# Attention at the head of a three-stage kernel: each unit's softmax weights are turned and used a step later, and GpSimd gets a written order

## The chip, the cores and the metric

One NeuronCore of a Trainium2 chip runs the whole program. The metric is the device time of one execution in microseconds (us). Engines are named as in the profile: PE (TensorE matmul), PEld (TensorE weight load), DVE (VectorE), ACT (ScalarE), POOL (GpSimd), SP (SyncE, which issues the DMAs here).

## The reference

Three stages in float32. Sizes: 4 batches, 8 heads, 576 positions, head size 64; then 2304 tokens of width 512, 8 experts of hidden width 1024, and a last layer of hidden width 2048.

```python
# attention: a window of 128 positions behind the query, with a slope per head
scores = q @ k.T / 8
mask = (rel >= 0) & (rel < 128)
scores = where(mask, scores - slope[h] * abs(rel), -1e9)
attn = softmax(scores); x = attn @ v
# mixture of experts: one expert per token, chosen by the largest logit
logits = x @ w_gate + modality_bias[modality_id]
e = argmax(logits); gate = softmax(logits)[e]
x = gate * (relu(x @ w1[e]) @ w2[e])
# last layer
h = x @ w_in; out = (h * cos(h)) @ w_out
```

## The kernel before

The change touches only the attention stage. Its work is cut into 36 units: 2 pairs of batches, 9 tiles of 128 rows each (the fifth of a pair holds the last 64 rows of both batches), 2 groups of four heads. Unit n goes through these parts, each a function:

- `load` (by `ahead`, seven units ahead) brings q, k and v by DMA from SP's queue. q and k lie in a pool of 7 buffers, v in the ring `vts` of 12 tiles.
- `tr` (four units ahead) transposes q and k on PE into a "T" bank (two banks). ACT copies the result (`qT`, `rT`), and POOL makes the high and low halves of k and the low half of q: three POOL instructions (L682 to L684). In the trace these transposes are `bk<-ident,rqk`.
- `score(n)` multiplies q and k on PE (`bk<-kT,qT`). Then DVE merges the diagonal block with its neighbour (L716), adds the bias and takes the minimum (L722), and ACT takes the exponential into `e` (L725). Units with s = 4 (8, 9, 26 and 27) hold three blocks of keys; their e is the tile `e1`, one buffer. The others have two buffers.
- `flip(n)` transposes e on PE (`bk<-ident,e`) into the one "P" bank. ACT copies it (L742), and for most units POOL cuts two triangles out of it with two affine selects (L746, L748) into `pT`.
- `pv(n)` multiplies pT and v on PE (`bk<-vt,pT`) into the one "O" bank. DVE divides by the row sums (L766, L767, L770). After the second head group the rows of x are stored.
- For every tile `xt_split` transposes x and splits it on ACT and DVE. For every second tile `logits` adds three calls: `products` (gate logits on PE, copied by ACT to `ls`), `choose` (two small transposes and a chain of eight small DVE instructions, the last of which writes `ohb`, L825), and `ranks` (seven tiny matmuls on `ohb`, then a DVE chain with the integer casts and shifts L255 to L259, and L218).

The loop over n issues, in one step: score(n), one call from the list `after`, tr(n+4), flip(n-1), pv(n-2), one more call from `after`. So choose runs in the first half of a step, and ranks in the second half of the same step. The class `Turns` makes PE keep this written order in steps 2 to 32; the order of the other engines is the scheduler's. In the first steps `setups` also issues the bias of the three-block units (POOL and DVE), the loads for routing (`load_route`, ten small DMAs, half-step 5), the integer tables (DVE casts of POOL's iotas, L602, half-step 8), and `setup_route` (half-step 11), in which PE transposes a tile `mf` that DVE casts just before.

Of the kernel before, what the change touches and what calls it, by code (L numbers as in the profile page):

```python
# [8 lines left out]
F32 = mybir.dt.float32  # L9
# [20 lines left out]
def kernel(  # L30
# [14 lines left out]
    nc = tc.nc  # L45
    B, H, S, D = q.shape
    NT, DM = out.shape
    NE, _, FF = w1.shape
# [10 lines left out]
    TE = T - 2  # L59
# [13 lines left out]
    def pool(c, name, bufs, side="left"):  # L73
        return c.enter_context(tc.tile_pool(name=name, bufs=bufs, side=side, reuse_waits="tile"))
# [93 lines left out]
    class Steps:  # L168


        def __init__(self, queue):
            self.queue, self.going = queue, []
# [306 lines left out]
    class Turns:  # L479


        on, last = False, None

        def __getattr__(self, name):
            op = getattr(tc.nc.tensor, name)

            def call(*args, **kwargs):
                with ExitStack() as c:
                    if self.on and self.last is not None:
                        c.enter_context(tc.issue_after(self.last.ins))  # L490
                    self.last = op(*args, **kwargs)  # L491
                return self.last

            return call

    class Ordered:

        sync, scalar, vector, gpsimd, tensor = nc.sync, nc.scalar, nc.vector, nc.gpsimd, Turns()

    nc = Ordered  # L500

    with ExitStack() as c:
# [3 lines left out]
        sm = pool(c, "sm", 5)  # L506
        vp = pool(c, "vp", 1)
# [137 lines left out]
        units = [(bp, s, hg) for bp in range(B // 2) for s in range(9) for hg in range(2)]  # L645
        N = len(units)
        R, KT, QT, X, ST, PT, O = {}, {}, {}, {}, {}, {}, {}
        vts = [vp.tile([128, 260], F32, name=f"vt{j}") for j in range(12)]

        def vt_of(bp, s, hg):  # L650
            return vts[(18 * bp + 2 * s + hg) % len(vts)]
# [34 lines left out]
        def score(n):  # L686
            bp, s, hg = units[n]
            t0, nt, bt, bc, f0, nv = window(s)
            if n < 2:
                nt = nv  # L690
            w, w0, wv = 128 * nt, 128 * f0, 128 * nv
            kT, qT = KT[bp, hg][:, :, :, 128 * t0:128 * t0 + w], QT.pop(n)
            nm = sm.tile([128, 4], F32, name="nm")
            e = sm.tile([128, 4, 128 * (3 if nv == 3 else 1)], F32, name="e%d" % (nv // 3), bufs=2 if nv < 3 else 1)

            def products(sc, pairs):


                for p in pairs:
                    for a, b in ((0, 0), (0, 1), (1, 0)):  # L700
                        for j in range(2):
                            rs = slice(64 * j, 64 * j + 64)
                            nc.tensor.matmul(sc[j][:, p - pairs[0], :w], qT[rs, a, p], kT[rs, b, p],
                                             start=a == 0 and b == 0, stop=a == 1)

            for pairs in ([0, 1],) if nv < 3 else ([0], [1]):
                if pairs[0]:
                    yield
                sc = [bank("S", [128, 2, 256] if nv < 3 else [128, 1, 512]) for j in range(2)]
                products(sc, pairs)  # L710
                for j in range(2):
                    if nv == 2:


                        own, other = (slice(128, 256), slice(0, 128)) if s < 4 else (slice(0, 128), slice(128, 256))
                        nc.vector.copy_predicated(sc[j][:, :, other], near.unsqueeze(1).to_broadcast([128, 2, 128]),  # L716
                                                  sc[j][:, :, own])
                        w0, wv, bc = other.start, 128, 0
                    for p in pairs:
                        h = 2 * p + j  # L720
                        x = sm.tile([128, 384], F32, name="sx")
                        MARK["dve"] = nc.vector.tensor_tensor_reduce(  # L722
                            out=x[:, :wv], in0=sc[j][:, p - pairs[0], w0:w0 + wv], in1=bt[:, 4 * hg + h, bc:bc + wv],
                            op0=ALU.add, op1=ALU.min, scale=-0.125, scalar=3.0e38, accum_out=nm[:, h:h + 1])
                        MARK["act"] = nc.scalar.activation(e[:, h, :wv], x[:, :wv], AF.Exp, bias=nm[:, h:h + 1],  # L725
                                                           scale=-1.0)
            ST[n] = (e, nv, t0 + f0)
            yield
# [27 lines left out]
        def pv(n):  # L756
            bp, s, hg = units[n]
            heads, t0 = PT.pop(n)
            ot = bank("O", [128, 4, 128])
            for h, pT in enumerate(heads):  # L760
                for b in range(len(pT)):
                    nc.tensor.matmul(ot[:, h, 0:65], pT[b], vt_of(bp, t0 + b, hg)[:, 65 * h:65 * h + 65],
                                     start=b == 0, stop=b == len(pT) - 1)
            t = 9 * bp + s
            den = sm.tile([128, 4], F32, name="den")
            nc.vector.tensor_scalar(den, ot[:, :, D], 1.0e-9, None, op0=ALU.add)  # L766
            nc.vector.reciprocal(den, den)  # L767
            if hg == 0:
                X[t] = gp.tile([128, DM], F32, name="y") if t >= TE else xp.tile([128, DM], F32, name="xt")
            nc.vector.tensor_tensor(  # L770
                X[t][:, 256 * hg:256 * hg + 256].rearrange("p (h d) -> p h d", d=D), ot[:, :, 0:D],
                den.unsqueeze(2).to_broadcast([128, 4, D]), op=ALU.mult)
            if hg == 1:
                with ExitStack() as w:
                    if t >= TE:
                        w.enter_context(tc.issue_after(MK["w"].ins))
                    nc.sync.dma_start(x_dram[128 * t:128 * t + 128, :], X[t])
                after.append(lambda: xt_split(t))
                if t % 2:
                    after.extend(logits(t - 1))  # L780
                if t == TE - 1:
                    after.extend(early())

        def xt_split(t):
            xT = xTs[(t // 2 + 1) % 2]
            c0 = 128 * (t % 2)
            pt = bank("T", [128, KD, 128])
            for kk in range(KD):
                nc.tensor.transpose(pt[:, kk], X[t][:, 128 * kk:128 * kk + 128], ident)
            nc.scalar.copy(xT[:, 0, :, c0:c0 + 128], pt)  # L790
            nc.vector.tensor_tensor(xT[:, 1, :, c0:c0 + 128], pt, xT[:, 0, :, c0:c0 + 128].bitcast(F32),
                                    op=ALU.subtract)
# [45 lines left out]
                rawc.close()  # L838
                RP.append(pool(bc, "rp", 2, "right"))

        LF, LP = 1, 2
        after = []
        for vt in vts:
            nc.vector.memset(vt.rearrange("p (h e) -> p h e", e=65)[:, :, D:65], 1.0)
        ahead(0, 3, 0)
# [6 lines left out]
            ahead(0, 5, 1)  # L852

        def setups(i):
            if i == 5:
                load_route()
            with behind("dve", "act", "pool"):
                if i == 4:
                    LATER.append(setup_bias(bias4))
                if i == 7:  # L860
                    todo.extend(LATER.pop())
                if i == 8:
                    for fn in tables:
                        fn()
                if i == 11:
                    setup_route()
                for fn in todo[:1 if i > 1 else 2]:
                    todo.pop(0)()

        def pops(count):  # L870
            for _ in range(count):
                if after:
                    after.pop(0)()

        LATER = []
        for n in range(N + LP):
            if n < 3:
                ahead(n, dt=n + 1)
            nc.tensor.on = 1 < n < 33
            scores = score(n) if n < N else iter(())  # L880
            next(scores, None)
            setups(2 * n)
            pops(1 if n < 33 else 2)
            if n > 1:
                ahead(n + 1)
            next(scores, None)
            flips = flip(n - LF) if LF <= n < N + LF else iter(())
            next(flips, None)
            setups(2 * n + 1)
            old = len(after)  # L890
            if n >= LP:
                pv(n - LP)
            next(flips, None)
            pops(min(old, 1) if n < 33 else 2 if n < N + LP - 1 else 1)

    nc = tc.nc
    banks(S=2, T=2, P=2, O=1)
# [131 lines left out]
    class InOrder:  # L1029


        on = False
# [18 lines left out]
    class Engines:  # L1051
        scalar, vector, gpsimd, tensor = (InOrder(e) for e in (nc.scalar, nc.vector, nc.gpsimd, nc.tensor))
        sync, values_load = nc.sync, nc.values_load

    nc = Engines
    with ExitStack() as c:
# [104 lines left out]
        for n in range(len(steps) + LAG):  # L1161
            InOrder.on = ORD <= n < ORE
            if n < len(steps):
                i, f = steps[n]
# [81 lines left out]
    with tc.If(n_units > 1):  # L1246
        with tc.For_i(1, n_units):
# [10 lines left out]
            parts = unit_parts()  # L1258
# [12 lines left out]
    with ExitStack() as c:  # L1271
# [16 lines left out]
        GG, ACC, LAST, PART, LP = {}, {}, [], {}, {0: (fp, 512)}  # L1288
# [63 lines left out]
        last = downs[-TAIL:]  # L1352
# [4 lines left out]
        fetches, loads, sums = {}, {}, {}  # L1357
        for s, (g, f0, f1) in enumerate(segs):
            i0 = order.index((s, f0))
            for j in range(groups[g][1]):  # L1360
                if s and (s == 1 or f0 == 0):
                    at = 0 if s == 1 else i0 - 8
# [67 lines left out]
```

## Time and profile before

| | |
|---|---|
| median of 3 runs | 869.53 us (868.23 to 871.9) |
| the profiled execution | 879.99 us, span 878.3 us |
| PE busy | 818.1 us (93%) |
| DVE busy | 615.6 us (70%) |
| ACT busy | 492.2 us (56%) |
| POOL busy | 198.7 us (23%) |
| mean granted PE clock | 0.965 of full |

Shares are of the span. Attention is the first 214 us or so; the two later stages fill the rest. The profiled execution is 10.5 us above the median of the unprofiled runs. A granted clock of 1.00 is 2.4 GHz and 0.5 is 1.2 GHz; a value between is a mean over a stretch that had both.

### The profile page before, as it was taken

The numbers are of one execution on the slowest core, as the hardware profiler recorded it, in microseconds if no ns is written. First come the engines' busy times: TensorE is split into PE (matmuls) and PEld (weight loads), VectorE is DVE, ScalarE is ACT, GpSimd is POOL, SyncE is SP. The second block draws the span as 40 slices with busy tenths as digits, with TensorE's granted clock in tenths as the row PEclk, the third lists the DMA queues.
The fourth block names the chain that finished last, engine by engine and source line by source line (L and its number), as shares of the span: only waits on it lengthen the run. The fifth ranks groups of instructions, "written<-read, shape, count | busy, mean of one in ns | idle before, by whom it ended". The sixth has DMA issues, their size and how long they took to land. (4 is left out here: it accounts for less than half of the span.)

```text
span 878.3 us, 14760 instructions
## 1 busy us (share of the span) xinstructions
PE 818.1 (93%) x5269; PEld 721.6 (82%) x5269; DVE 615.6 (70%) x1461; ACT 492.2 (56%) x912; POOL 198.7 (23%) x259
## 2 busy tenths in 40 slices
PE   7788888998879999999899999999999999999996
PEld 6677877886879999999897877788788888888895
DVE  3853656665888999999474998898656565555562
ACT  6454555654355667666454676675454555445562
POOL 5542546351012213233000212111404000200000
PEclk9697999997999999999989999999999999999999
DMA  8443443104378888877844223140403000100000
GB/s 172 105 113 83 102 104 91 44 26 163 115 234 285 270 279 280 279 251 237 282 147 129 88 71 118 59 169 0 138 20 106 4 0 10 64 1 0 25 26 24
DMA packets 125136, 103.41 MB, mean 118 GB/s; under 512 B 61726, under 2 KB 105028, under 8 KB 125060
## 3 DMA queue, kind: packets, MB, share of 16 engines
q1 hardware_dynamic: 122099, 92.74, 35.1%
q0 software_dynamic: 2960, 9.70, 3.1%
q8 instruction: 42, 0.69, 0.3%
q14 instruction: 35, 0.28, 0.1%
HBM read 85.90 MB, written 16.52 MB: 117 GB/s over the span
## 5 line engine op out<-in xcount | busy, mean ns | idle before, releaser
L1044 PE MATMUL bk<-hh,s 128*128 128x256 f32 x864 | 119.8, 287 | 9.4 <-ACT y L1044 4.5
L1044 PE MATMUL bk<-xT,s 128*128 128x256 f32 x864 | 116.7, 285 | 4.4 <-ACT xT L1044 2.2
L1044 PEld LDWEIGHTS bk<-hh,s 128*128 128x128 f32 x864 | 110.2, 192 | 11.4 <-DVE y L1044 5.2
L1044 PEld LDWEIGHTS bk<-xT,s 128*128 128x128 f32 x864 | 108.9, 191 | 5.3 <-DVE s L1044 2.3
L1044 POOL TENSOR_TENSOR lf<-lf,mag 128x512 f32<-128x512 f32 x32 | 47.7, 1491 | 287.2 <-DVE mag L1044 262.5
L1044 ACT CAST s<-r 128x1024 fp32r<-128x1024 f32 x72 | 75.2, 1051 | 59.9 <-DMA r<-in_moe_w_dram 40.7
L1044 DVE TENSOR_TENSOR s<-r,s 128x1024 fp32r<-128x1024 f32 x72 | 94.1, 1309 | 18.6 <-ACT s L1044 18.3
L1044 PE MATMUL bk<-yT,wi_a 128*128 128x512 f32 (+1 forms) x480 | 104.3, 368 | 1.2 <-DVE yT L1044 0.8
L1044 PE MATMUL bk<-yT,wi_b 128*128 128x512 f32 (+1 forms) x480 | 105.0, 368 | 0.0
L1044 ACT ACTIVATE r<-r 128x512 f32<-128x512 f32 (+1 forms) x80 | 47.2, 590 | 93.5 <-DVE r L1044 93.5
L1044 PEld LDWEIGHTS bk<-yT,wi_a 128*128 128x128 f32 x480 | 84.0, 189 | 17.1 <-DVE yT L1044 1.1
L1044 PEld LDWEIGHTS bk<-yT,wi_b 128*128 128x128 f32 x480 | 84.7, 188 | 15.7
L1044 PE MATMUL bk<-wo_b,gg 128*128 128x512 f32 x384 | 93.2, 391 | 1.8 <-DVE po L1044 1.1
L1044 DVE TENSOR_TENSOR r<-bk,r 128x512 f32<-128x512 f32 (+1 forms) x80 | 51.0, 637 | 61.6 <-ACT r L1044 61.0
L1044 PE MATMUL bk<-wo_a,gg 128*128 128x512 f32 x384 | 92.4, 389 | 0.5 <-DVE gg L1044 0.5
L1044 PEld LDWEIGHTS bk<-wo_b,gg 128*128 128x128 f32 x384 | 71.6, 188 | 18.2 <-issue 1.3
L1044 PEld LDWEIGHTS bk<-wo_a,gg 128*128 128x128 f32 x384 | 71.9, 188 | 15.9 <-DVE gg L1044 1.0
L491 PE MATMUL bk<-vt,pT 128*128 128x65 f32 x544 | 72.9, 290 | 7.4 <-POOL pT L748 4.2
L491 PEld LDWEIGHTS bk<-vt,pT 128*128 128x128 f32 x544 | 70.5, 208 | 9.5 <-POOL pT L748 5.4
L1044 DVE TENSOR_TENSOR gg<-r,gg 128x512 fp32r<-128x512 f32 x64 | 46.3, 723 | 34.3 <-ACT gg L1044 34.3
L725 ACT ACTIVATE e<-sx,nm 128x128 f32<-128x128 f32 (+1 forms) x144 | 50.2, 420 | 22.9 <-DVE nm L722 16.6
L1044 ACT CAST gg<-r 128x512 fp32r<-128x512 f32 x64 | 39.7, 620 | 41.1 <-DVE r L1044 39.1
(282 smaller groups left out, 1288.9 us busy)
## 6 DMA issues: line engine op xcount, KB each, us to landing
r<-in_moe_w_dram SPq DMA_DIRECT2D x72, 512.0 KB
y_dram<-y SPq DMA_DIRECT2D x19, 256.0 KB
rqk<-in_q_dram SPq DMA_DIRECT2D x32, 128.0 KB
rqk<-in_k_dram SPq DMA_DIRECT2D x32, 128.0 KB
vt<-in_v_dram SPq DMA_DIRECT2D x32, 128.0 KB
x_dram<-xt SPq DMA_DIRECT2D x16, 256.0 KB
f64x<-in_moe_w_in_dram SPq DMA_DIRECT2D x8, 512.0 KB
raw<-in_moe_w_dram SPq DMA_DIRECT2D x8, 512.0 KB
```

Of the source, the lines that this page charges most:

```text
L491: self.last = op(*args, **kwargs)
L725: MARK["act"] = nc.scalar.activation(e[:, h, :wv], x[:, :wv], AF.Exp, bias=nm[:, h:h + 1], scale=-1.0)
L1044: r = op(*args, **kwargs)
```

## The change

- flip(n) moves to step n+2, ahead of tr, and pv(n) to step n+3. The last units are brought forward again (`turned`, `summed`): from step 33 on they are as close behind their scores as before. So step 32 holds flips 30 and 31, and step 33 holds pv 30 and 31.
- In the body of the stage, xt_split and the calls of `logits` get written steps (`later`): xt_split at the head of the step after pv, products at the end of that step, choose in the first half of the next, ranks at the end of the one after.
- The class Turns now wraps GpSimd too: from step 2 to 33 POOL keeps the order in which its instructions are written.
- Buffers: e 3 in place of 2, e1 2 in place of 1, vts 14 in place of 12.
- `load_route` is issued at half-step 3 in place of 5, and `setup_route` at 13 in place of 11.

```diff
     class Turns:
-        on, last = False, None
+        on = False
+        def __init__(self, eng):
+            self.eng, self.last = eng, None
...
-        sync, scalar, vector, gpsimd, tensor = nc.sync, nc.scalar, nc.vector, nc.gpsimd, Turns()
+        sync, scalar, vector, gpsimd, tensor = nc.sync, nc.scalar, nc.vector, Turns(nc.gpsimd), Turns(nc.tensor)
...
-        vts = [vp.tile([128, 260], F32, name=f"vt{j}") for j in range(12)]
+        vts = [vp.tile([128, 260], F32, name=f"vt{j}") for j in range(14)]
...
-            e = sm.tile([128, 4, 128 * (3 if nv == 3 else 1)], F32, name="e%d" % (nv // 3), bufs=2 if nv < 3 else 1)
+            e = sm.tile([128, 4, 128 * (3 if nv == 3 else 1)], F32, name="e%d" % (nv // 3), bufs=3 if nv < 3 else 2)
...
+                p = 2 * t + 2 + LP
+                if t < TE - 2:
+                    later(p, 0, lambda: xt_split(t))
+                else:
+                    after.append(lambda: xt_split(t))
                 if t % 2:
-                    after.extend(logits(t - 1))
+                    calls = logits(t - 1)
+                    if t < TE - 2:
+                        later(p, 1, calls[0])
+                        later(p + 1, 0, calls[1])
+                        later(p + 2, 1, calls[2])
+                    else:
+                        after.extend(calls)
...
-        LF, LP = 1, 2
+        LF, LP = 2, 3
...
-            if i == 5:
+            if i == 3:
                 load_route()
...
-                if i == 11:
+                if i == 13:
                     setup_route()
...
+        END = N - 4
+        turned = [n + LF for n in range(N)]
+        summed = [n + LP for n in range(N)]
+        for n in range(END - 2, N):
+            turned[n] = max(n + 1, END)
+            summed[n] = max(n + 2, END + 1)
+        for n in range(N + 2):
...
+            Turns.on = 1 < n <= END + 1
             scores = score(n) if n < N else iter(())
             next(scores, None)
             setups(2 * n)
-            pops(1 if n < 33 else 2)
+            calls(due.pop((n, 0), []))
...
+            flips = [flip(m) for m in range(N) if turned[m] == n]
+            for p in flips[:1]:
+                next(p, None)
             if n > 1:
                 ahead(n + 1)
-            next(scores, None)
-            flips = flip(n - LF) if LF <= n < N + LF else iter(())
-            next(flips, None)
+            run(scores)
             setups(2 * n + 1)
-            if n >= LP:
-                pv(n - LP)
-            next(flips, None)
+            sums = [m for m in range(N) if summed[m] == n]
+            for m in sums[:1]:
+                pv(m)
+            for p in flips:
+                run(p)
+            for m in sums[1:]:
+                pv(m)
+            calls(due.pop((n, 1), []))
```

## Rows read from the trace of the kernel before

**Rows 1.** Three stretches: busy of each engine (x instructions), PE clock, DMA share, GB/s.
```profile
0.00:46.00 46.00, 35.76 (x235) 30.19 (x237) 27.57 (x132) 27.57 (x74) 23.49 (x62) 0.85 0.67 139
46.00:206.00 160.00, 142.00 (x1247) 126.56 (x1248) 93.12 (x500) 88.02 (x227) 71.00 (x119) 0.93 0.30 77
214.00:878.00 664.00, 635.44 (x3748) 560.31 (x3747) 491.04 (x806) 374.17 (x609) 102.11 (x77) 0.99 0.39 125
```

**Rows 2.** PE's waits, 46 to 206 us: total us, times, longest.
```profile
PE bk L491 <- DVE ohb L825: 10.5, 6, 2.0
PE bk L491 <- ACT rT L681: 1.7, 1, 1.7
PE bk L491 <- ACT pT L742: 1.5, 2, 0.8
PE bk L491 <- POOL pT L748: 1.4, 5, 0.5
PE bk L491 <- DVE xT L791: 1.0, 2, 0.6
PE bk L491 <- DMA vt<-in_v_dram: 0.9, 1, 0.9
PE bk L491 <- POOL pT L746: 0.8, 1, 0.8
```

**Rows 3.** Timeline of PE: start, us, what, in brackets the idle time before.
```profile
77.92 1.65 PE L491 MATMUL bk<-kT,qT 64*128 64x256 f32 x12
...
99.27 0.97 PE L491 MATMUL bk<-kT,qT 64*128 64x256 f32 x12
...
105.05 0.18 PE L491 MATMUL bk<-ohb,tri 128*128 128x8 bf16 x1 [1.81 <-DVE ohb L825]
```

**Rows 4.** Two of five stretches with a fallen clock, columns as in rows 1.
```profile
70.00:82.00 12.00, 12.00 (x72) 10.83 (x70) 3.06 (x17) 2.90 (x8) 1.79 (x5) 0.57 0.12 27
...
143.00:149.00 6.00, 5.10 (x41) 4.95 (x42) 4.30 (x24) 2.49 (x7) 0.73 (x2) 0.72 0.32 92
```

**Rows 5.** Timeline around a unit with three blocks.
```profile
64.55 2.13 ACT L725 ACTIVATE e<-sx,nm 128x384 f32<-128x384 f32 x4 [1.59 <-issue]
...
67.21 0.66 PE L491 MATMUL bk<-ident,e 128*128 128x128 f32 x4 [0.82 <-ACT pT L742]
...
69.61 0.81 PE L491 MATMUL bk<-ident,e 128*128 128x128 f32 x4 [1.74 <-ACT rT L681]
```

**Rows 6.** Timeline of the first steps, all engines.
```profile
22.15 0.60 SPq L561 DMA_DIRECT2D wr<-in_moe_w_gate_dram  x1
...
23.45 0.60 PE L491 MATMUL bk<-ident,rqk 128*128 128x128 f32 x4
...
24.53 5.63 DVE L602 CAST rev<-ints 128x8 f32<-128x8 int32 x1
...
25.82 0.25 SPq L571 DMA_DIRECT2D mi<-in_moe_modality_id_dram  x1
...
27.25 2.10 PE L491 MATMUL bk<-vt,pT 128*128 128x65 f32 x16 [2.77 <-POOL pT L748]
...
29.48 0.65 POOL L748 TENSOR_SCALAR_AFFINE_SELECT pT<-pa 128x512 f32<-128x512 f32 x1
...
35.52 0.29 PE L491 MATMUL bk<-ident,mf 18*128 18x18 f32 x1 [2.05 <-DVE mf L577]
```

**Rows 7.** POOL's groups, 46 to 206 us: busy, mean ns of one, idle before.
```profile
L683 POOL TENSOR_TENSOR kT<-rT,kT 128x256 fp32r<-128x256 f32 x26 | 19.1, 734 | 0.1
...
L748 POOL TENSOR_SCALAR_AFFINE_SELECT pT<-pa 128x512 f32<-128x512 f32 x21 | 13.4, 637 | 0.0
...
L682 POOL TENSOR_SCALAR kT<-rT 128x256 fp32r<-128x256 f32 x25 | 10.2, 407 | 73.2 <-ACT rT L681 71.6 <-PE bk L491 1.5
```

**Rows 8.** One of the casts of ranks on DVE, 46 to 206 us.
```profile
L255 DVE CAST ri<-rank 128x2 int32<-128x2 f32 x7 | 1.2, 170 | 0.0
```

**Rows 9.** Timeline of PE at the end of attention.
```profile
208.66 0.33 PE L491 MATMUL bk<-ident,y 128*128 128x128 f32 x1 [1.58 <-DVE y L770]
```

More of the change, by code (lines that the diff above doesn't have):

```diff
@@ L479 @@
     class Turns:
-        on, last = False, None
+        on = False
+        def __init__(self, eng):
+            self.eng, self.last = eng, None
         def __getattr__(self, name):
-            op = getattr(tc.nc.tensor, name)
+            op = getattr(self.eng, name)
             def call(*args, **kwargs):
                 with ExitStack() as c:
-                    if self.on and self.last is not None:
+                    if Turns.on and self.last is not None:
                         c.enter_context(tc.issue_after(self.last.ins))
@@ L777, in pv @@
                     nc.sync.dma_start(x_dram[128 * t:128 * t + 128, :], X[t])
-                after.append(lambda: xt_split(t))
-                if t % 2:
-                    after.extend(logits(t - 1))
+                p = 2 * t + 2 + LP
[3 more added lines that the diff above has]
+                    after.append(lambda: xt_split(t))
+                if t % 2:
+                    calls = logits(t - 1)
[5 more added lines that the diff above has]
+                        after.extend(calls)
                 if t == TE - 1:
@@ L839, in ahead, with later @@
                 RP.append(pool(bc, "rp", 2, "right"))
-        LF, LP = 1, 2
-        after = []
+        LF, LP = 2, 3
+        after, due = [], {}
+        def later(step, at, fn):
+            due.setdefault((step, at), []).append(fn)
         for vt in vts:
@@ L868, in setups, with calls, run @@
                     todo.pop(0)()
[L870 to L873, printed above, removed]
-        LATER = []
-        for n in range(N + LP):
+        def calls(fns):
+            while fns:
+                fns.pop(0)()
+        def run(parts):
+            for _ in parts:
+                pass
+        LATER = []
+        END = N - 4
[5 more added lines that the diff above has]
+        for n in range(N + 2):
             if n < 3:
                 ahead(n, dt=n + 1)
-            nc.tensor.on = 1 < n < 33
+            Turns.on = 1 < n <= END + 1
             scores = score(n) if n < N else iter(())
@@ L882 @@
             setups(2 * n)
-            pops(1 if n < 33 else 2)
+            calls(due.pop((n, 0), []))
+            if n > END:
+                calls([after.pop(0) for _ in after[:2]])
+            flips = [flip(m) for m in range(N) if turned[m] == n]
+            for p in flips[:1]:
+                next(p, None)
             if n > 1:
                 ahead(n + 1)
-            next(scores, None)
-            flips = flip(n - LF) if LF <= n < N + LF else iter(())
-            next(flips, None)
+            run(scores)
             setups(2 * n + 1)
-            old = len(after)
-            if n >= LP:
-                pv(n - LP)
-            next(flips, None)
-            pops(min(old, 1) if n < 33 else 2 if n < N + LP - 1 else 1)
+            sums = [m for m in range(N) if summed[m] == n]
[6 more added lines that the diff above has]
+            calls(due.pop((n, 1), []))
+            if n > END:
+                calls([after.pop(0) for _ in after[:2 if n < N + 1 else 1]])
+        assert not due
     nc = tc.nc
```

## The prediction

> **What bounds the kernel now.** I read the busy times by stretch first [rows 1]. Behind 214 us PE is busy 635 of 664 us at a granted clock of 0.99; the change touches nothing there, so that part only shifts in time. In attention, from 46 to 206 us, PE is busy 142 of 160 us; the next engine, DVE, has 93 us, ACT 88, POOL 71. So PE sets the pace there, and two things make its 160 us longer than its work: 18 us without work, and a clock of 0.93.
>
> PE's waits in the same stretch [rows 2] add up to 17.8 us, the whole idle time. 10.5 us of it is six waits of ranks' first matmul on `ohb`. One of them in the timeline [rows 3]: the unit's scores start at 99.27, products with v follow, and then PE stands still for 1.81 us until 105.05. Choose and ranks are in one step, and choose's chain on DVE stands partly behind the division of that step's products, so PE, which keeps its written order, waits for it.
>
> The clock second [rows 4]. A stretch with a mean of 0.72 over 6 us spent 56% of it, 3.4 us, at 1.2 GHz; 0.57 over 12 us is 10.3 us. There are four stretches of the first size and one of the second: 23.9 us at the lower level. Each begins behind waits of 1 to 2.6 us: three behind a wait for `ohb`, the long one behind the pair of [rows 5], one behind waits for v and pT. Twelve score matmuls take 1.65 us in the slow stretch and 0.97 us at full clock [rows 3], so 41% of slow time is lost: 23.9 x 0.41 = 9.8 us.
>
> The first 46 us are different [rows 1]: PE busy 35.8 us, clock 0.85 (13.8 us at the lower level), and the waits are for start-up work.
>
> **The change part by part.**
>
> *Ranks a step and a half behind choose.* `ohb` is then ready some 6 us before it is wanted; the six waits go, -10.5 us. What is late next is not PE: ranks add 0.3 us of matmuls as before. On DVE the chain of ranks now runs while POOL works. In every one of the six waits of before, POOL was idle by then, because PE had stood still. The cast of ranks took 170 ns there [rows 8]. A cast that began while POOL worked without a gap took 5.63 us, and ended with POOL's last instruction, 24.53 + 5.63 against 29.48 + 0.65 [rows 6]. So the new cost per group of ranks lies between 0 and 5.6 us of DVE. POOL's burst in a step is two selects and three halves of q and k [rows 7] (the second select costs as the first, q's half as k's): 2 x 0.64 + 0.41 + 2 x 0.73 = 3.2 us. It starts with ACT's copy of the turned e, by my count 2.6 us into the step, and ends at 5.8, while the casts come at about 5.0. So 0.8 us on DVE, and I charge half to PE: six groups x 0.4 = +2.4 us. Bounds 0 and 34.
>
> The Trainium skill bears on this (SBUF — State Buffer, "Who interferes with whom"): DVE in its two-port modes, which casts can enter, and GpSimd share one port pair, and whichever issues second waits for the other's whole instruction. By that rule each of the four casts and shifts loses at most one POOL instruction, 4 x 0.73 = 2.9 us a group, and the sum would be up to 15 us worse. The trace agrees that they exclude each other, but the long cast sat through nine POOL instructions, not one.
>
> *Flip two behind, pv three behind, flip ahead of tr, more buffers.* pT is cut a whole step before it is used: its waits go (1.4 + 0.8 = 2.2 us). The ring of 14 v tiles gives a load two steps behind the product that frees its tile, in place of one: -0.9. Around the three-block units the exponentials stood 1.59 us until the one e1 was turned, and ACT's copies behind them held PE 0.82 and 1.74 us [rows 5]; the second e1 buffer takes that away. But xt_split, one third of the flip and tr want three "T" banks in one step and there are two. So of 1.7 + 1.5 + 1.0 = 4.2 us I let 2.0 stay: -2.2. Together -5.3 us; bounds -2 and -7.3.
>
> *POOL in written order.* Each select is written ahead of k and q of the same step; k is needed two to four steps later. A step of PE lasts 4 to 6 us and POOL has 3.2 us, so nothing queued behind a waiting select is wanted in time; 0 us, bounds 0 and +5 (a late pT or k once in a while).
>
> *Clock.* With the waits go the falls behind them. I keep two short ones, 2 x 3.4 x 0.41 = 2.8 us: 9.8 - 2.8, -7.0 us. Bounds -9.8 and 0.
>
> *The end.* From step 33 on the order is as before, but pv(31) follows pv(30) at once, and there is one O bank, which DVE must divide out. A wait of PE for that division at the end of attention is 1.58 us [rows 9], with more in front of it; I take +1.0, bounds 0 and 1.6. The lag adds no work: the same matmuls run.
>
> *The first six steps.* For: pv's wait for pT, 2.77 us at 27.25 [rows 6], goes. Against: the ten routing loads held SP from 22.15 to 26.07, 3.9 us; they now stand ahead of the twelve loads of units 8 and 9. tr(8), at 23.45 before, gets its data up to 3.9 us later, and PE comes to it earlier; 0 to 3.9 us. Also pv(1) now falls in the step of the integer casts. Its division stands on DVE behind the 5.63 us cast, xt_split(0) waits for that division at the head of step 5, and PE in order behind xt_split: 0 to 5.4 us. The wait for `mf` (2.05 us) moves a step on and stays. POOL runs the bias selects ahead of the halves of later units, which are not due: 0. The clock there is low before and, with such waits, will be again. Sum: 0 us, bounds -6 and +7.
>
> *Sum.* -10.5 - 5.3 - 7.0 + 2.4 + 1.0 + 0 = -19.4 us, on the profiled execution's 879.99 us: 860.6. That execution is 10.5 us above the median; the same 19.4 us from 869.53 give 850.1 us. Adding the bounds would give a far wider span than is likely, since they don't come together. Layout of memory behind attention may shift the hand-over by 2 us or so either way.
>
> **Rivals.**
>
> A. The start eats a third of it. The cast is starved longer because POOL's backlog is longer, xt_split(0) and tr(8) both wait, and the clock stays low: +7 us. For it: [rows 6] show the starving and the order is written out. Against: pv's wait goes at the same place. Time: 857.
>
> B. More than forecast: the start gains 6 us (pT's wait gone, casts not starved), and no fall of the clock stays (2.8 us). Time: 841.
>
> C. No change: PE loses its waits, but another engine takes the pace, as DVE, whose order the scheduler sets, holds the score banks. Then only some 3 us come back. For it: DVE is the next engine. Against: 93 of 160 us is far from full [rows 1]. Time: 867.
>
> D. Slower. The place is DVE in ranks, the mechanism the starving of [rows 6]: every one of six groups meets a POOL that, now in written order and no longer stopped by PE's waits, has no gap, and stands 5.63 us. The scores wait for their banks, PE falls idle that long, and each time the clock falls (3.4 x 0.41 = 1.4 us). Price 6 x 7.0 = 42 us in place of 2.4, with the 7.0 us of clock already in it given up: about +27 us net, 896. It decides from 3.2 us a group: below that the gain of 19.4 + 2.4 = 21.8 us, shared by six and less the falls, is not used up. Against: POOL is busy 71 of 160 us, and its burst is 3.2 us long, so only a backlog could hold a cast for longer.
>
> That the change does nothing: POOL's order and the lag are written into the instruction streams, so the order itself will change; only its effect can fail, which is C.
>
> **How the numbers follow.** The forecast, 850 (its own range 844 to 856): 0.50. A 0.22, B 0.14, C 0.08, D 0.06. Within 0.5% is 865.2 to 873.9 us, about what a measurement can tell from no change here. Faster holds the forecast, A and B: 0.86. Same is C: 0.08; slower is D: 0.06. For 8 in 10 the range takes in A and most of B and leaves out C and D: 838 to 862.
>
> **What would show it.** Right: between step 7 and step 32 PE has no wait for `ohb`, pT from POOL, or v; PE's busy share there is 95% or more at a clock of 0.97 or above; attention ends 15 to 25 us earlier, and the time behind it is as long as before. The casts L255 to L259 show longer times than 170 ns where POOL is busy. The flips of units 9 and 27 still show about 1 us. In the first steps I expect waits for the q and k loads of unit 8, for DVE at xt_split(0), and for `mf`.
>
> Wrong: DVE's `ri` casts of some us with PE waiting for `bk` behind them (D); scores waiting for DVE in every step (C); an attention stage as long as before with PE busy at full clock, which would mean that I read its work as shorter than it is.

## The result, and the profile after

The changed kernel takes 842.9 us (median of 4 runs, 841.54 to 844.73), the kernel before beside it 870.71 us (4 runs, 868.23 to 874.11): a ratio of 0.968, 95% interval 0.964 to 0.972, or 27.8 us less. The forecast was 850.1 us, with a range of 838 to 862.

I cut each profiled execution at three marks on PE: the first gate-logit product (end of the start), the first transpose of `y` (end of the middle), and the first product of the second stage. Columns are as in [rows 1]. The kernel before:

```profile
0.00:44.82 44.82, 34.58 (x225) 29.35 (x226) 26.80 (x129) 26.39 (x72) 22.89 (x60) 0.85 0.67 137
44.82:206.26 161.44, 143.44 (x1260) 127.66 (x1259) 94.08 (x504) 89.46 (x230) 71.61 (x120) 0.93 0.30 78
206.26:222.49 16.23, 9.80 (x65) 7.67 (x64) 8.55 (x33) 6.00 (x11) 2.13 (x2) 0.68 0.81 261
222.49:878.30 655.81, 630.31 (x3725) 556.91 (x3725) 486.17 (x796) 370.39 (x603) 102.11 (x77) 0.99 0.38 123
```

The changed kernel:

```profile
0.00:43.82 43.82, 35.36 (x241) 29.69 (x242) 25.33 (x141) 29.24 (x80) 26.32 (x65) 0.92 0.72 151
43.82:176.86 133.04, 128.97 (x1236) 116.09 (x1235) 93.62 (x485) 87.28 (x222) 70.54 (x115) 1.00 0.35 91
176.86:192.46 15.60, 10.03 (x72) 7.48 (x71) 9.54 (x41) 5.23 (x9) 2.13 (x2) 0.67 0.73 250
192.46:843.00 650.54, 627.06 (x3725) 552.50 (x3725) 486.24 (x798) 370.34 (x604) 102.24 (x77) 1.00 0.38 124
```

The middle falls from 161.4 to 133.0 us, by 28.4. Its second column says how: PE's busy time falls by 14.5 us, and what is left of the stretch, PE's idle time, from 18.0 to 4.1. The clock is 1.00 throughout. The other stretches change by -1.0, -0.6 and -5.3 us; the last of these is not the change's (below, "Both kernels once more"). The list of PE's waits that answers to [rows 2], 46 to 178 us of the changed kernel (total us, times, longest), is now whole with two rows:

```profile
PE bk L494 <- DVE xT L804: 2.1, 3, 1.0
PE bk L494 <- DVE xt L773: 1.8, 2, 1.4
```

`xT` is the split copy of x, whose making holds a T bank; `xt` is x as DVE divides it. No wait for `ohb`, pT, rT or v is left.

Less busy time for the same work is the clock. PE's groups in the middle, before first (operation, shapes, count, busy us, mean ns, idle before):

```profile
L491 PE MATMUL bk<-vt,pT 128*128 128x65 f32 x466 | 60.3, 284 | 3.2 <-POOL pT L748 1.4 <-DMA vt<-in_v_dram 0.9 <-POOL pT L746 0.8
L491 PE MATMUL bk<-ident,e 128*128 128x128 f32 x148 | 24.3, 290 | 3.9 <-ACT rT L681 1.7 <-ACT pT L742 1.5 <-DVE xT L791 0.6
```

and after:

```profile
L494 PE MATMUL bk<-vt,pT 128*128 128x65 f32 x466 | 55.9, 273 | 0.0
L494 PE MATMUL bk<-ident,e 128*128 128x128 f32 x148 | 22.6, 279 | 0.0
```

The six forms with equal counts lose 9.0 us between them (these two 4.4 and 1.7). The two whose counts differ by a few (`kT,qT` and the transposes of q and k) lose 2.9 us at equal work. That makes about 12.0 us by the clock. The other 2.4 of the 14.5 us are 24 matmuls that now fall outside the marks, 16 of them ahead of the first and 8 behind the second.

### The profile page after: what moved, and what is told of

It reads as the page before. It is cut to its first block, busy times and chain, and to the rows that moved or that the text cites. A ratio compares the mean times of both kernels' runs of the same rounds, so it can differ in the third digit from the quotient of the medians.

```text
span 843.0 us, 14736 instructions
## 1 busy us (share of the span) xinstructions
PE 801.4 (95%) x5269; PEld 705.8 (84%) x5269; DVE 614.7 (73%) x1463; ACT 492.1 (58%) x912; POOL 201.2 (24%) x259
## 5 line engine op out<-in xcount | busy, mean ns | idle before, releaser
L1079 PE MATMUL bk<-hh,s 128*128 128x256 f32 x864 | 117.7, 284 | 7.8 <-DVE y L1079 4.6
L1079 PEld LDWEIGHTS bk<-hh,s 128*128 128x128 f32 x864 | 107.8, 188 | 10.1 <-DVE y L1079 5.6
L1079 PE MATMUL bk<-xT,s 128*128 128x256 f32 x864 | 114.5, 282 | 1.7 <-DVE s L1079 1.1
L1079 DVE TENSOR_TENSOR s<-r,s 128x1024 fp32r<-128x1024 f32 x72 | 94.3, 1313 | 13.6 <-ACT s L1079 13.2
L494 PE MATMUL bk<-vt,pT 128*128 128x65 f32 x544 | 66.8, 276 | 0.1
L494 PEld LDWEIGHTS bk<-vt,pT 128*128 128x128 f32 x544 | 65.1, 195 | 1.2 <-issue 1.0
L1079 DVE SCALAR_TENSOR_TENSOR r<-ki,bk 128x512 f32<-128x512 int32 (+1 forms) x80 | 50.4, 630 | 16.5 <-ACT ki L1079 15.9
```

What stands on the lines that cost most here:

```text
L1079: r = op(*args, **kwargs)
```

## Experiments

All twelve were timed beside the kernel before; ratios are to it. "Middle" is the stretch cut as above, in one profiled execution of each kernel. How finely they read is shown by the kernel before itself, run once more: 1.005 (1.001 to 1.008). So a difference under 1% between two of them is not taken for one.

**Both kernels once more.** No edit.

> The kernel before once more. Theory: the profile shown first was a slow execution of it by 10.5 us, with a mean clock of 0.965; a repeated profile gives its middle at 155 to 162 us and the stage behind it at 650 to 655, the waits for ohb again six at 9 to 12 us, and the count of falls of the clock differs. Rival: the same 161.4 and 655.8 within 1 us, then the profiled excess over the median is an effect of profiling.

> The changed kernel once more, in the same call. Measures what a repeated profile gives for the stretches: if the stage behind attention of 650.5 us in the changed kernel's profile and 655.8 in that of before is run-to-run spread (theory), this gives some value between 649 and 656 with no change of its waits; if it is the change (rival: layout of memory or later start of transfers), 650 to 651 again. Middle 133 within 1 us, time 842 to 847.

Measured: before 875.29 us (869.2 to 883.56), changed 847.77 us (840.58 to 852.57), ratio 0.971 (0.966 to 0.976). The four stretches of the kernel before, run again:

```profile
0.00:41.40 41.40, 32.37 (x225) 27.02 (x226) 26.43 (x129) 26.22 (x72) 22.90 (x60) 0.92 0.69 145
41.40:201.26 159.86, 144.15 (x1260) 129.10 (x1259) 94.06 (x504) 89.38 (x230) 71.58 (x120) 0.91 0.31 80
...
216.43:867.50 651.07, 628.71 (x3725) 554.23 (x3725) 487.24 (x796) 370.61 (x603) 103.00 (x77) 0.99 0.38 124
```

and of the changed kernel, run again:

```profile
43.89:176.97 133.08, 129.02 (x1236) 116.11 (x1235) 93.67 (x485) 87.64 (x222) 70.56 (x116) 1.00 0.36 93
...
192.55:850.90 658.35, 633.96 (x3725) 559.54 (x3725) 486.16 (x798) 371.18 (x604) 102.32 (x77) 0.98 0.38 123
```

The middles repeat: 161.4 and 159.9 before, 133.0 and 133.1 after. The stage behind attention does not: 650.5 and 658.3 us in one and the same kernel, of which 6.9 us are PE's busy time (627.06 and 633.96) at a lower clock. So the -5.3 us there is spread, as both expectations had it, and the spread is wider than they said: 658.3 lies beyond the 649 to 656 that I gave it. Against the repeated profile of before, the changed kernel's first differs by +2.4 in the start, -26.8 in the middle, +0.4 and -0.5 behind it. The gain is the middle: 26.8 to 28.4 us, and the medians differ by 27.8, in the second pair of runs by 25.0.

**The ranks' lag alone.** To the kernel before:

```diff
-                    after.extend(logits(t - 1))
+                    calls = logits(t - 1)
+                    after.extend(calls[:2])        # for t < TE - 2
+                    due[2 * t + 6] = calls[2]      # issued at the end of that step
```

> The kernel before, with one edit: ranks run a step and a half behind choose. Theory (PE's stops and the clock falls behind them): the six waits for ohb, 10.5 us, go, and with them the three short clock falls behind them, 3 x 3.4 x 0.41 = 4.2 us; 14.7 us faster than before, no PE wait for ohb in the trace. Rival (the stop only moves: PE then stands for pT, which had been made ready during the ohb waits): 5 us or less faster, with the waits for pT from GpSimd grown from 2.2 us to over 8.

**All but the ranks' lag.** To the changed kernel:

```diff
-                        later(p + 2, 1, calls[2])
+                        later(p + 1, 1, calls[2])
```

> The changed kernel, with one edit undone: ranks run half a step behind choose again. Theory: six waits of 1 to 2 us for ohb come back (10.5 us) and up to three short clock falls (4.2 us); 10 to 15 us slower than the changed kernel. Rival (with the flip ahead of tr and pv a step later, the DVE chain of choose no longer stands behind that step's division, so the wait is short anyway): 4 us slower or less.

Measured: ranks' lag alone 864.42 us (856.78 to 871.06), 0.989 (0.984 to 0.994), middle 147.8. All but it 862.5 us (856.3 to 873.9), 0.989 (0.984 to 0.995), middle 147.5. PE's waits with the ranks' lag alone, in its middle:

```profile
PE bk L491 <- ACT rT L681: 3.5, 2, 1.7
PE bk L491 <- POOL pT L748: 1.7, 3, 1.3
PE bk L491 <- ACT pT L742: 1.6, 2, 0.8
PE bk L491 <- POOL pT L746: 1.5, 2, 1.1
```

and without it, 46 to 190 us:

```profile
PE bk L494 <- DVE ohb L838: 8.3, 6, 1.9
PE bk L494 <- DVE xT L804: 2.9, 3, 1.8
```

Each half takes away its own waits and leaves the other's. With the ranks' lag alone the six waits go, as theory had it, but the time falls by 8.6 us and not by 14.7. Some of the stop moves, as the rival had it, though far less: the waits for GpSimd's pT are 3.2 us in place of 2.2, not over 8. Without the ranks' lag the six waits are back, and the kernel takes 14.7 to 19.6 us more than the changed one, against 10 to 15 in theory. In the middle they add up: -13.6 and -13.9 against -28.4 for both. The medians do not: 8.6 and 10.5 us sum to 19, the whole change brought 25 to 28. Each half keeps falls of the clock whose number differs from run to run, but no run shows that this makes the difference, so it stays open. The second half was tried only as a whole: the flip ahead of tr, and the written steps of xt_split, products and choose, were not undone by themselves.

**The buffers.** Three kernels: the buffers alone on the kernel before; the changed kernel with the old ones; the changed kernel with only the old e buffers. The edit of the first; the others undo both lines of it, and the second alone:

```diff
-        vts = [vp.tile([128, 260], F32, name=f"vt{j}") for j in range(12)]
+        vts = [vp.tile([128, 260], F32, name=f"vt{j}") for j in range(14)]
...
-                        name="e%d" % (nv // 3), bufs=2 if nv < 3 else 1)
+                        name="e%d" % (nv // 3), bufs=3 if nv < 3 else 2)
```

> The kernel before with the changed kernel's buffers alone: e 3, e1 2, vts 14; order as before. Theory (each half of the change pays by a wait and the clock behind it): the buffers take away only the wait for v (0.9 us) and, around the three-block units, the exponentials' 1.59 us and the two waits of 0.82 and 1.74 behind them, with a clock fall of up to 10.3 us x 0.41 = 4 us: 3 to 7 us faster, the six ohb waits (10.5 us) stay; middle from 161 to 154 to 158 us. Rival 1 (what the lagged turn brought is all in the buffers, since with the old e buffers the lag brought nothing): 14 us, middle 147, as with the lag. Rival 2 (a buffer more moves nothing while flip stays one step behind): within 2 us of before.

> The changed kernel, with the buffers of before (e 2, e1 1, vts 12). Theory: with the flip two steps behind, a second exponential now waits for the flip of the unit two before it; ACT stands for e and PE for what ACT copies: e and e1 together cost 5 to 15 us, and vts about 1 us. Rival (the flip comes early enough in its step, ahead of the exponentials, so e needs no third buffer): only the three-block units wait, 2 to 3 us slower.

> The changed kernel with the tiles of e as before (2, and 1 for the three-block units) and the 14 tiles of v kept. Theory 1 (the third buffer matters only around the three-block units, because the flip stands ahead of the exponentials in its step): the stretch from the first gate products to the end of attention takes 133 us plus the waits of units 9 and 27 and one long clock fall, 4 to 9 us more; elsewhere no PE wait for a copy of pT. Theory 2 (the lag brings nothing without its buffers): 12 to 15 us more in that stretch, as with all old buffers (13.7), spread over all steps.

In the second kernel, with 12 v tiles and the products three steps behind, some v tiles are overwritten before their last product; its output is not the reference's. Measured: buffers alone 872.69 us, 0.998 (0.994 to 1.003), middle 160.4. Old buffers 863.26 us, 0.991 (0.987 to 0.994), middle 146.7. Old e buffers alone 859.55 us, 0.982 (0.977 to 0.987), middle 150.8, in an execution of 867.09 us, the slowest of its six. PE's waits with the buffers alone, from 46 us on, against [rows 2]:

```profile
PE bk L491 <- DVE ohb L825: 10.2, 6, 1.9
PE bk L491 <- DVE xT L791: 2.7, 3, 1.6
PE bk L491 <- POOL pT L746: 0.7, 1, 0.7
PE bk L491 <- POOL pT L748: 0.6, 2, 0.5
```

The waits for v, rT and ACT's pT are gone, as theory had it, and xT's is longer by 1.7. PE's idle time in the middle falls from 18.0 to 14.5 us, but the clock there is 0.90, and no time comes of it. Rival 2 holds for the time. With the lag and the old e buffers alone, PE stands again where it stood in [rows 5], now for ACT's pT and then for the T bank that `xT` holds:

```profile
65.80 1.65 PE L494 MATMUL bk<-ident,e 128*128 128x128 f32 x8 [1.84 <-ACT pT L745]
68.18 1.11 PE L494 MATMUL bk<-ident,rqk 128*128 128x128 f32 x4 [0.73 <-DVE xT L804]
69.08 5.22 PE L494 MATMUL bk<-vt,pT 128*128 128x65 f32 x24
```

In the changed kernel these 24 products take 2.79 us. The same comes again at unit 27, and elsewhere the old e buffers add no wait, as theory 1 had it: PE's idle time in the middle is 7.6 us against 4.1. The time is nearer to theory 2: this middle is 17.8 us longer, 14.2 us of it busy time at a clock of 0.90. Not all of that is the buffers' doing, since one of its three falls of the clock stands behind a wait for `xt` that the changed kernel has too, without a fall (last section). With all the old buffers the clock fell behind the two pairs alone, and the middle is 13.7 us longer. So the lag's half of the gain needs the e buffers: without them the middle, 146.7 and 150.8 us, is no shorter than with the ranks' lag alone (147.8). The waits stand where e1 is used; the third e was not tried apart from the second e1. And the buffers need the lag: alone they take waits away, but no time.

**POOL's order.** The changed kernel with GpSimd left to the scheduler, and the kernel before with GpSimd's order written (by the changed class Turns). The edit of the first:

```diff
-  vector, gpsimd, tensor = nc.vector, Turns(nc.gpsimd), Turns(nc.tensor)
+  vector, gpsimd, tensor = nc.vector, nc.gpsimd, Turns(nc.tensor)
```

> The changed kernel, with GpSimd's order left to the scheduler again. Theory: the order is worth nothing in the steady steps, since pT and k are wanted steps later: within 2 us of the changed kernel, no PE wait for GpSimd. Rival (without the order GpSimd puts the halves of later units ahead of the selects): PE waits for pT from GpSimd by 4 us or more, and 4 to 10 us slower.

> The kernel before with GpSimd's written order alone. Without the order the changed kernel took 5.2 us longer up to the first gate products, and the same time behind. Theory (in the first steps GpSimd's written order leaves a gap between k's high and low half, where DVE's cast of the tables comes through): the cast of 5.63 us takes under 2.5 us here, and the first gate products come 2 to 5 us earlier than 44.8. Rival (the order pays only with the flip ahead of tr): the cast stays over 4 us, and the first gate products come at 44 us or later. Behind them both expect 161 us give or take 4.

Measured: order left free 848.96 us (845.52 to 853.78), 0.974 (0.970 to 0.978), middle 133.3. Order alone 881.84 us (873.51 to 887.76), 1.008 (1.005 to 1.012), middle 168.7 with pT waits of 4.3 us in place of 2.2. In the start with the order left free, first the first integer cast on DVE:

```profile
24.66 2.43 DVE L605 CAST rev<-ints 128x8 f32<-128x8 int32 x1
```

then PE's wait for xt_split(0) and the products behind it:

```profile
30.12 0.44 PE L494 MATMUL bk<-ident,xt 128*128 128x128 f32 x2 [3.12 <-DVE xt L773]
...
31.97 3.52 PE L494 MATMUL bk<-vt,pT 128*128 128x65 f32 x16
```

The cast is 0.47 us in the changed kernel and its wait 1.70. So the order shortens one wait by 1.4 us in the start and does nothing in the middle, where PE has no wait for GpSimd without it either, as theory had it. The start ended at 49.0 us against 43.8 with the same idle time of PE (8.3 and 8.5 us): the 5 us are busy time at a clock of 0.83 in place of 0.92. The kernel with the old e buffers, whose start has POOL's order written and no new wait, had 47.1 at 0.82. With the order alone the cast takes 0.17 us and the start ends at 42.1, as theory had it; but the kernel before itself ends its start at 44.8 and at 41.4 with a cast of 5.6 us both times, so the start doesn't tell what the cast costs. The middle of 168.7 lies beyond the 161 give or take 4 of both its theory and its rival, at a clock of 0.89. In time the order is worth nothing that these runs resolve.

**Routing loads and tables.** The changed kernel with `load_route` and `setup_route` at their old half-steps 5 and 11; the kernel before, and the changed kernel, with the integer casts at half-step 1 in place of 8. The edit of the last two:

```diff
-                if i == 8:
+                if i == 1:
                     for fn in tables:
```

> The changed kernel with load_route and setup_route at their old half-steps (5 and 11). Theory 1 (the move cost the wait for unit 8's loads and gained nothing): the wait of 0.75 us for q and k of unit 8 goes, the wait for mf (1.3 us) stays, a step earlier: within 1.5 us of the changed kernel. Theory 2 (at half-step 11 the casts for the routing stand right behind the table casts, and the loads they need land late): PE waits for mf by 3 us or more, and 3 to 6 us slower.

> The kernel before, with the integer tables cast on DVE in half-step 1 in place of 8, when GpSimd has nothing to do. Theory (the 5.63 us of the first cast are GpSimd's doing, and DVE's lateness holds PE at 31.5 and 35.5 us): the cast takes under 0.3 us; the waits of PE for xT and mf shrink by 1 to 2.5 us and the first gate products come 1 to 4 us earlier than 44.8. Rival (PE waits for pT at that place anyway): under 1 us earlier.

> The changed kernel with the ten integer casts and the three small instructions behind them issued at half-step 1 in place of 8. Theory: PE's wait of 1.70 us for xt_split(0) comes from the division queued behind these casts, so it goes, and nothing else does: 1 to 2 us faster than the changed kernel at L0, middle unchanged at 133. Rival 1: the division is late by itself (it is short of pv's products by no cast), the wait stays, time within 1 us. Rival 2: the casts before the scores delay DVE's first bias, PE waits there instead: 0 to 2 us slower.

Measured: old half-steps 850.37 us (844.78 to 855.69), 0.971 (0.965 to 0.976). Casts early on the kernel before 874.68 us, 0.997 (0.992 to 1.001); on the changed kernel 843.48 us (840.5 to 845.05), 0.967 (0.964 to 0.971). With the old half-steps PE's wait for the loads of unit 8 is gone and the one for `mf` is 1.6 us, a step earlier, as theory 1 had it. The first cast takes 0.17 us when it is early, on a POOL that had not begun its bursts. On the kernel before, the start then ends at 42.7 us, inside the 41.4 and 44.8 of that kernel without an edit. In the changed kernel the wait for xt_split(0) goes, another comes at the transposes behind it, and the one at the transpose of `mf` grows from 1.27 us:

```profile
27.84 0.72 PE L494 MATMUL bk<-ident,rqk 128*128 128x128 f32 x4 [0.55 <-ACT xT L803]
...
34.05 0.20 PE L494 MATMUL bk<-ident,mf 18*128 18x18 f32 x1 [1.82 <-DVE wg L578]
34.19 3.56 PE L494 MATMUL bk<-vt,pT 128*128 128x65 f32 x16
```

Of the 1.7 us that went, 1.1 are given back at these two, and the clock falls behind the second; the start ends 0.6 us earlier. None of the three moves is resolved in time, so the version with early casts is no better than the changed kernel as far as these runs tell.

## Why the prediction was right, point by point

The direction and the main steps were right, and the time lies in the range. The size was 8.4 us too small (19.4 forecast, 27.8 measured; 5.6 against the 25.0 of the second pair), and one term, the clock, carries most of that. By its own steps, against the first profile of before:

- *Ranks.* -10.5 forecast: the six waits went, idle time of the middle -13.9 in all, for which the steps (-10.5 - 5.3 + 2.4) give -13.4. Undoing this part alone brought six waits of 8.3 us back.
- *The casts beside POOL.* 0.8 us on DVE and 0.4 on PE per group were forecast. DVE's instructions of ranks, in the changed kernel, 46 to 178 us:

```profile
L218 DVE TENSOR_TENSOR ob<-iota,pf 128x256 f16<-128x256 f16 x7 | 4.3, 611 | 0.1
L257 DVE TENSOR_SCALAR ph<-ri 128x2 int32<-128x2 int32 x7 | 2.7, 389 | 0.2
L259 DVE CAST pf<-ph 128x4 f16<-128x4 int32 x7 | 2.4, 344 | 0.1
L255 DVE CAST ri<-rank 128x2 int32<-128x2 f32 x7 | 1.3, 183 | 0.0
```

  Before, the four took 3.1, 1.2, 1.2 and 1.2 us (the last is [rows 8]): 4.0 us more in seven groups, 0.6 each. Where ranks stood one step earlier they were short again (3.0, 1.2, 1.2 and 1.1), though two small additions in front of them (L252 and L253) took 234 and 407 ns there, against 156 each before. PE's longest wait in the middle is 1.44 us for xt_split, behind a division that DVE reached after L259 (0.58 us) and L218 (0.82 us), together 0.8 us longer than before; with one more it makes the 1.8 us of "DVE xt" where 2.4 was forecast. With ranks one step earlier that row is absent from PE's waits. Rival D needed 3.2 us a group by its text; with the 1.4 us that it charges for each fall, (21.8 - 6 x 1.4) / 6 gives 2.2. The 0.6 measured is under both.

  How a cast stands beside POOL shows in the timeline of the changed kernel:

```profile
77.27 0.73 POOL L494 TENSOR_TENSOR kT<-rT,kT 128x256 fp32r<-128x256 f32 x1
...
77.40 0.62 DVE L257 TENSOR_SCALAR ph<-ri 128x2 int32<-128x2 int32 x1
...
77.95 0.73 POOL L494 TENSOR_TENSOR qT<-rT,qT 128x256 fp32r<-128x256 f32 x1
...
78.12 0.58 DVE L259 CAST pf<-ph 128x4 f16<-128x4 int32 x1
```

  L257 ends at 78.02, with POOL's instruction (78.00), and L259 at 78.70, with the next (78.68). Each began while that POOL instruction ran, and ended with it. The Trainium skill (SBUF — State Buffer, "Who interferes with whom") says that whichever of the two issues second waits for the other's whole instruction. Here the trace agrees, with ends that lie 0.02 us apart; the 5.63 us of [rows 6] the rule does not explain. I had weighed that row as the upper bound, and the bound was not reached.

- *Lag and buffers.* Waits for pT, v, rT and ACT's pT gone; of the T banks' waits 2.0 us were to stay, 1.8 stayed (0.81 and 0.98 at units 9 and 27; the other 0.3 of the `xT` row is the gate products' wait for their input). That the e buffers take the long pair away is shown from both sides.
- *The clock*, the mis-sized term: -7.0 forecast, -12.0 measured. The factor came from score products (1.65 against 0.97 us, 41% lost). The products with v lose more. Two lots of 24 in the kernel before, one in the slow stretch of [rows 4] and one as it ends:

```profile
70.21 5.22 PE L491 MATMUL bk<-vt,pT 128*128 128x65 f32 x24
...
80.92 2.79 PE L491 MATMUL bk<-vt,pT 128*128 128x65 f32 x24
```

  That is 47%, and 23.9 x 0.47 = 11.2 us. And the two falls that I kept (2.8 us) did not stay, though waits of 1.44, 0.98 and 0.81 us did. These make 4.2 of the missing 5.0 us; 0.8 is not located. This was rival B's second half, and I had given B 0.14; its first half, 6 us in the start, did not come, so that 842.9 lies near B's 841 is in part chance. How much clock there was to win varies too: added up from stretches of 1 us, the middle of before had 23.9 us at 1.2 GHz in one profile and 27 in the other. The middle of the changed kernel had none in both profiles, nor with GpSimd's order free or the casts early; with the old half-steps it had one fall of 3.4 us.
- *POOL's order.* 0 forecast; 0.3 us in the middle, and nothing resolved in all.
- *The end.* +1.0 forecast, -0.6 measured (+0.4 against the repeated profile): within what two profiles of one kernel differ by. The wait that I charged did not come: PE's waits for `y` there are 0.5 us in place of 3.6, but it waits 1.9 for `oa`, a tile of the routing.
- *The first six steps.* 0 forecast, -1.0 and +2.4 against the two profiles of before, with 16 matmuls more done by the mark. The waits came where they were named, each at the low side. PE, changed kernel:

```profile
23.43 0.41 PE L494 MATMUL bk<-ident,rqk 128*128 128x128 f32 x2 [0.51 <-DMA rqk<-in_q_dram]
...
28.31 0.67 PE L494 MATMUL bk<-ident,xt 128*128 128x128 f32 x2 [1.70 <-DVE xt L773]
...
36.20 0.20 PE L494 MATMUL bk<-ident,mf 18*128 18x18 f32 x1 [1.27 <-DVE mf L580]
```

  The first was put at 0 to 3.9 us, the second at 0 to 5.4, the third at 2.05. The second is short because the cast that held DVE for 5.63 us in [rows 6] takes 0.47.
- *The stage behind attention* was to keep its length. It does, within a spread of 8 us in one and the same kernel, where I had allowed for 2 us.
- *The signs.* PE is busy for 97% of the middle at a clock of 1.00, as named. Attention ended 29.4 us earlier than in the first profile of before, more than the 15 to 25 named, and 24.4 earlier than in the second.

## What to carry to other kernels

Where PE keeps a written order and stands a little in every step, the price of a wait is the wait and the fall of the clock that can follow: here 13.9 us idle and 12.0 us of clock. Size the second from the operation that fills the slow stretches, not from another. A lag and the buffers that feed it are one edit: without the buffers the same unit stops PE again, and the buffers without the lag took waits away here but brought no time.

Two profiles of each kernel before a term is believed: a stage that the change doesn't touch moved by 8 us here, and only repeating the kernel told that from the change.

## What the runs showed of the hardware that was not expected

- A short wait does not always bring a fall of the clock. The changed kernel keeps 1.00 through waits of up to 1.44 us. The kernel with all but the ranks' lag waits for `ohb` 1.63 us until 73.50, 1.91 until 111.64 and 1.92 until 128.95; its stretches around these (PE busy, clock, DMA share, GB/s):

```profile
74.00:84.00 10.00, 10.00 (x74) 0.71 0.32 81
...
104.00:114.00 10.00, 7.86 (x81) 1.00 0.54 138
114.00:124.00 10.00, 10.00 (x101) 1.00 0.48 119
124.00:134.00 10.00, 8.09 (x82) 1.00 0.25 67
134.00:144.00 10.00, 10.00 (x86) 1.00 0.19 54
```

  The shortest of the three has a fall behind it, the longer two have none. The same wait in the same kernel can go either way: in the kernel before, those for `ohb` of 1.09 and 1.81 us (until 84.80 and 105.05) had no fall behind them in the first profile, and those of 1.12 and 1.81 us at the same places had one in the second. So can the same wait in two kernels. First PE's wait for `xt` in the changed kernel, which keeps 1.00; then the stretch behind the same wait (1.43 us until 123.77) with the old e buffers:

```profile
114.49 0.44 PE L494 MATMUL bk<-ident,xt 128*128 128x128 f32 x2 [1.44 <-DVE xt L773]
...
124.00:134.00 10.00, 10.00 (x55) 0.51 0.25 67
```

  The length of the wait alone does not decide. What does is open.
- The same cast of 128 x 8 integers took 5.63, 2.43, 0.47 and 0.17 us: in the kernel before, with the changed order but POOL left to the scheduler, in the changed kernel, and issued ahead of POOL's bursts. A hold of one POOL instruction (0.84 us at most in the start of before) covers the last two, not the first two. The two long ones end within 0.03 us of the end of a run of POOL instructions without a gap (30.16 against 30.13 us, and 27.09 against 27.06). In all six profiles with POOL's order written and the cast at half-step 8 it took 0.16 to 0.55 us, beside a POOL that has gaps of some 0.1 us between the halves of k (24.27 + 0.45 against 24.81 in the changed kernel). So the written order does shorten this cast; that the gaps do it is likely, not shown.
